# Delta rule and expert layer: first inverse evicted from PSUM by partition quarters, states and scaled values on ScalarE, a new planned order

## The chip, the cores and the metric

The kernel runs on one core of a Trainium2 chip. The metric is device time in microseconds (us) of one execution, as the median of several runs; lower is better. A profiled execution is a separate run in which every instruction's start and end is recorded. It takes a little longer, so its times are compared with its own sum.

The core has a matrix engine (TensorE, PE in the profile; its weight loads are PEld), VectorE (DVE), ScalarE (ACT), GpSimd (POOL) and SyncE (SP). Each engine takes its instructions strictly in the order of its own queue. SP is used here to issue transfers (DMA), as are ScalarE's and GpSimd's queues at places. TensorE's results land in PSUM, 128 partitions with eight banks each, and are copied from there to SBUF by ScalarE or VectorE; such a copy is called an eviction below.

## The reference

Two blocks follow each other, all in float32.

```python
# delta rule: q, k, v are (4, 8, 768, 48), beta is (4, 8, 768)
k_n = k / (norm(k) + 1e-6)
state = zeros((B, H, D, D))
for t in range(S):
    y[:, :, t] = einsum('bhd,bhde->bhe', q[:, :, t], state)
    v_old = einsum('bhde,bhd->bhe', state, k_n[:, :, t])
    state = state + beta[t] * einsum('bhd,bhe->bhde', k_n[:, :, t], v[:, :, t] - v_old)
# experts: x is y with heads joined, (3072, 384); each row goes to the one expert with the largest logit
expert = argmax(x @ w_gate, axis=1); gate = softmax(x @ w_gate)[expert]
out[row] = gate * (relu(x[row] @ w1[expert]) @ w2[expert])   # 8 experts, hidden size 1024
```

## The kernel before

**Tiling.** The 768 steps of a sequence are cut into NT = 12 chunks of C = 64. One *turn* t handles chunk t of all 32 heads at once. Within a chunk the recurrence is a triangular system, so a turn needs the inverse of a unit-like triangular 64 x 64 matrix per head. That inverse is built from two 32 x 32 diagonal blocks (by VectorE) and one block across them (by TensorE).

**Scores.** `scores(t)` multiplies keys with keys and queries with keys. For t >= 2 it does this in two halves of 32 products each (L323, written "half a" and "half b" below), into the PSUM pair BY, which ScalarE evicts into XY (keys with keys, tile blkA) and P (queries with keys, tile pA) before the next half can start. For t < 2 the keys' product comes first, into BY for t = 0 and BZ for t = 1, and is evicted to XY by ScalarE (first bank) and VectorE (second bank); the product with the queries follows later. `dve(1024, ...)` at L355 multiplies P by a mask on VectorE.

**The inverse.** `invert(n)` serves the turns 2n and 2n + 1. Four DMAs copy the diagonal blocks of XY, one 32-partition quarter each, into tile GD (also in blkA); for n = 0 two of them are issued by SP and two by ScalarE. VectorE transposes GD into GL (L378, two instructions), computes norms and factors by Newton steps (L386 to L413; the last writes nt, the inverse norms per token), then does the elimination (L417 to L450, some 95 small instructions) and two transposes into TT (L458). `tmp`, `prod`, `X` and U are its scratch tiles.

**A turn.** `load_kv(t)` loads v and kt and scales v by nt: for t < 2 with 16 ScalarE instructions (L473), else with one VectorE instruction of 768 elements (L476). `turn(t)` puts v into the PSUM pair BR (`values`, L520), adds the state's part (`with_state`, L502), evicts it as R (ScalarE), multiplies with the diagonal blocks (`inverse(0)`, L537), evicts Z (ScalarE), adds the part across (L547), evicts R, multiplies again (`inverse(1)`), evicts Z, and adds keys times Z to the state in PSUM (`kz`, L561). The state is evicted in two halves of 64 partitions each, one by ScalarE and one by VectorE (recorded at L257 and L259, the lines of the helper `copy`), into S, for the next turn. `output(t)` and `logits(t)` compute the chunk's result, store it, and compute the router's logits; `route` computes each row's place in its expert's list, mostly with small VectorE instructions, and scatters the places to HBM.

**Experts.** `early_rows`, `early`, `expert(e)` gather rows by those lists, transpose them (L830), do both layers (L848, L877) and scatter the result. Three weight buffers overlay tiles of the first block (blkA, pA), so the first expert's weights are loaded once the inverses are done.

**The order.** Nothing is ordered by the order of the source. `P.op(engine, cost, fn, r, w, prio, passes)` records a work item with its engine, an assumed cost, what it reads and writes, and a due time (`prio`, in turns). `Plan.order` then replays the items with these costs on a model of the engines: at each step the engine that is free first takes, of what is ready, the item with the lowest due time; items with a due time of at most URGENT (R, Z and S copies) are waited for if they are about to come. LAT is the assumed delay from one engine to another. [...] The instructions are issued in the resulting order, so a changed cost can move any of them on any queue. The Tile layer sets the semaphores from the tiles that the instructions touch.

## Time and profile before

| | us |
|---|---|
| median of 3 runs | 600.73 (600.27 to 600.76) |
| the profiled execution | 616.37 |
| its span, first to last instruction | 614.6 |
| PE busy | 516.0 (84%) |
| DVE busy | 241.7 (39%) |
| ACT busy | 151.2 (25%) |
| mean granted TensorE clock | 0.893 |

How to read it: the span is what the records cover; the profiled execution's own time is 1.8 us longer. Busy time is an average over two quite different parts. Up to about 287 us the turns run, after that the experts. "Idle before" in a timeline line stands in square brackets: how long the engine had done nothing, and which instruction's end let it go on. The list of waits has the columns who waited, for whom, us in total, times, longest. A group line gives line, engine, operation, output and input, shapes, count, busy us and mean ns of one, and idle time before.

### The profile page before, as it was taken

How to read it: one execution, taken by the hardware profiler on the slowest of the kernel's cores; microseconds unless marked ns; L12 is line 12 of the kernel's file. 1: busy time of each engine (PE TensorE's matmuls, PEld its weight loads, DVE VectorE, ACT ScalarE, POOL GpSimd, SP SyncE). 2: the span in 40 equal slices, each digit the busy share in tenths (PEclk: the TensorE clock that was granted, in tenths of full speed). 3: DMA queues.
4: the chain of work that ended last, by engine and by line, in shares of the span. 5: the costliest groups of instructions: out<-in, count | busy, mean ns of one | idle time of the engine just before them, and what ended most of it. 6: DMA issues, size and time to landing. Idle time of an engine off the chain costs nothing. (4 is left out here: it accounts for less than half of the span.)

```text
span 614.6 us, 15547 instructions
## 1 busy us (share of the span) xinstructions
PE 516.0 (84%) x6724; PEld 348.6 (57%) x6725; DVE 241.7 (39%) x957; ACT 151.2 (25%) x297; POOL 111.7 (18%) x118
## 2 busy tenths in 40 slices
PE   3447877889888888868869999999999999999990
PEld 3335665767767777756547455555555555555550
DVE  5795797978979874203101102101021011110100
ACT  2373443544445243321001111101101110101100
POOL 9000000030110301133042302213031130102011
PEclk9975786878969798865988999999999999999996
DMA  7985442434512245011755423314244220000000
GB/s 156 217 200 136 124 121 66 137 97 131 140 34 75 90 149 190 29 28 26 284 192 162 151 103 129 123 57 153 103 152 132 99 77 14 28 1 27 13 22 16
DMA packets 29511, 64.32 MB, mean 105 GB/s; under 512 B 5558, under 2 KB 17766, under 8 KB 29408
## 3 DMA queue, kind: packets, MB, share of 16 engines
q1 hardware_dynamic: 24368, 52.76, 28.7%
q0 software_dynamic: 4416, 9.47, 4.9%
q10 hardware_dynamic: 656, 1.07, 0.8%
q8 instruction: 53, 0.87, 0.6%
q14 instruction: 18, 0.15, 0.1%
HBM read 49.62 MB, written 11.04 MB: 99 GB/s over the span
## 5 line engine op out<-in xcount | busy, mean ns | idle before, releaser
L848 PE MATMUL pair<-kqA,blkA 128*128 128x416 f32 (+2 forms) x288 | 91.6, 477 | 3.2 <-ACT kqA L857 1.6
L877 PE MATMUL pair<-blkA,kqA 128*128 128x384 f32 x240 | 80.0, 491 | 0.0
L848 PEld LDWEIGHTS pair<-kqA,blkA 128*128 128x128 f32 x288 | 55.0, 205 | 37.2 <-issue 28.6
L854 DVE TENSOR_SCALAR kqA<-pair 128x416 f32<-128x416 f32 (+2 forms) x36 | 19.6, 544 | 140.8 <-PE pair L848 85.6
L777 POOL DMA_INDIRECT out<-y,rows_i x30 | 28.9, 962 | 222.0 <-ACT y L868 157.7
L323 PE MATMUL pair<-kqA 48*64 48x128 f32 (+1 forms) x896 | 40.5, 329 | 31.8 <-ACT pA L257 17.2
L877 PEld LDWEIGHTS pair<-blkA,kqA 128*128 128x128 f32 x240 | 45.0, 190 | 34.7 <-issue 5.6
L323 PEld LDWEIGHTS pair<-kqA 48*64 48x64 f32 x896 | 31.9, 181 | 37.8 <-ACT pA L257 17.1
L848 PE MATMUL pair<-kqA,pA 128*128 128x416 f32 x144 | 51.1, 514 | 0.3 <-ACT y L868 0.3
L857 ACT ACTIVATE kqA<-pair 128x416 f32<-128x416 f32 (+2 forms) x36 | 17.2, 478 | 134.0 <-PE pair L848 92.4
L537 PE MATMUL pair<-R,blkA 32*32 32x48 f32 x1536 | 34.4, 241 | 16.8 <-ACT R L257 8.2
L877 PE MATMUL pair<-pA,kqA 128*128 128x384 f32 x144 | 48.1, 491 | 0.0
L865 DVE TENSOR_SCALAR y<-pair,rows 32x384 f32<-32x384 f32 (+1 forms) x15 | 8.5, 607 | 92.8 <-ACT y L868 85.4
L537 PEld LDWEIGHTS pair<-R,blkA 32*32 32x32 f32 x1536 | 29.2, 150 | 22.2 <-ACT R L257 10.1
L848 PEld LDWEIGHTS pair<-kqA,pA 128*128 128x128 f32 x144 | 27.1, 190 | 22.7 <-issue 21.1
L877 PEld LDWEIGHTS pair<-pA,kqA 128*128 128x128 f32 x144 | 26.9, 190 | 21.2 <-issue 3.8
L502 PE MATMUL pair<-S,kqA 112*64 112x96 f32 x704 | 35.3, 259 | 2.8 <-ACT pA L257 1.8
L868 ACT ACTIVATE y<-pair,rows 128x384 f32<-128x384 f32 x15 | 8.7, 580 | 113.9 <-PE pair L877 108.3
L702 POOL DMA_INDIRECT lists<-ent,ri x24 | 24.9, 1038 | 63.2 <-DVE ri L690 27.4
L502 PEld LDWEIGHTS pair<-S,kqA 112*64 112x64 f32 x704 | 32.0, 145 | 4.5 <-ACT pA L257 2.4
L770 POOL DMA_INDIRECT kqA<-xs,rows_i x30 | 29.8, 994 | 24.1 <-DVE rows_i L767 15.3
L257 ACT ACTIVATE blkA<-pair 128x512 f32<-128x512 f32 x22 | 23.3, 1057 | 26.3 <-PE pair L323 24.0
(121 smaller groups left out, 673.6 us busy)
## 6 DMA issues: line engine op xcount, KB each, us to landing
kqA<-in_kq SPq DMA_DIRECT2D x46, 192.0 KB, 4.6
blkA<-in_w SPq DMA_DIRECT2D x15, 512.0 KB, 5.1
blkA<-in_w SPq DMA_DIRECT2D x10, 768.0 KB, 14.4
v<-in_vtok SPq DMA_DIRECT2D x12, 384.0 KB
kt<-in_ktok SPq DMA_DIRECT2D x12, 384.0 KB, 5.5
xs<-x SPq DMA_DIRECT2D x24, 192.0 KB, 2.3
pA<-in_w SPq DMA_DIRECT2D x9, 512.0 KB, 5.4
pA<-in_w SPq DMA_DIRECT2D x6, 768.0 KB, 4.6
```

Source lines behind the costliest of these rows:

```text
L257: return lambda: nc.scalar.activation(out=o, in_=i, func=AF.Copy, scale=scale)
L323: nc.tensor.matmul(bk[bank + e][half(x), i * w : i * w + w].rearrange("p (k c) -> p k c", c=C), lhsT=v[feat(e), 0, x * FQ + f, :], rhs=v[f ...
L502: nc.tensor.matmul(bk[bank + g][half(x ^ g if first else x), 2 * D * i : 2 * D * i + 2 * D], lhsT=KQ(t)[0 : 64 + D, k, x * FQ + f, :], rhs ...
L537: nc.tensor.matmul(at(BZ, f, e)[quad(q)], lhsT=tt[quad(q), :, 16 * u + 8 * e + f], rhs=R[quad(q), f, e, :], start=True, stop=True, skip_gr ...
L702: P.op("POOL", 1.0, lambda i=i: nc.gpsimd.indirect_dma_start(out=lists[i % 2], out_offset=bass.IndirectOffsetOnAxis(ap=ri[:, i : i + 1], a ...
L770: nc.gpsimd.indirect_dma_start(out=dst, out_offset=None, in_=xs, in_offset=bass.IndirectOffsetOnAxis(ap=idx, axis=0), bounds_check=N - 1, ...
L777: nc.gpsimd.indirect_dma_start(out=out, out_offset=bass.IndirectOffsetOnAxis(ap=idx, axis=0), in_=src, in_offset=None, bounds_check=N - 1, ...
L848: nc.tensor.matmul(bk[b][:, 0:n], lhsT=a1[:, s, f * 128 : f * 128 + 128], rhs=xT[:, s, :], start=(s == 0), stop=(s == NK - 1))
L854: (lambda f=f, b=b: nc.vector.tensor_scalar(out=hT[:, f, :], in0=bk[b][:, 0:n], scalar1=0.0, scalar2=None, op0=OP.max))
L857: (lambda f=f, b=b: nc.scalar.activation(out=hT[:, f, :], in_=bk[b][:, 0:n], func=AF.Relu)),
L868: (lambda: nc.scalar.activation(out=y[0:n], in_=bk[b][0:n, 0:DM], func=AF.Copy, scale=gate)),
L877: nc.tensor.matmul(bk[b][:, 0:DM], lhsT=hT[:, f, at : at + 128], rhs=a2[:, f, :], start=(f == 0), stop=(f == NF - 1))
```

## The change

- **First inverse.** For t < 2 the diagonal blocks are evicted straight from PSUM into GD by four instructions of 32 partitions and 512 elements, quarters 0 and 1 by ScalarE, 2 and 3 by VectorE. The four DMAs of `invert(0)` are gone. The evictions into XY for t < 2 remain, all on ScalarE, and are due later (t - 60 instead of t - 94).
- **cnt.** The copy of the constant `first` into cnt moves from VectorE to ScalarE.
- **Scaling of v.** For every turn it is done by 16 ScalarE instructions of 48 elements, each an item of its own, due at t - 1.5 (VP).
- **States.** Both halves of S are evicted by ScalarE.
- **The planner.** It knows a clock: within windows of 3.413 us it adds up how much of TensorE's array is used (`use`), and an item in a window after a slack one costs `cold` times as much. An order dependency (a write after a read) between instructions of one engine has no delay, VectorE's assumed delay is 0.12 instead of 0.16, and several costs differ. So the order changes on all engines.

```diff
+VP = 1.5
+WINDOW, WAKE, STAY = 3.413, 1000, 700
...
-    LAT = {"PE": 0.16, "DVE": 0.16, "ACT": 0.12, "POOL": 0.12, "SP": 2.0}
+    LAT = {"PE": 0.16, "DVE": 0.12, "ACT": 0.12, "POOL": 0.12, "SP": 2.0}
...
+            order.update(self.readers.get(k, ()))
...
+        deps += [(d, 0.0 if self.ops[d][0] == eng and eng != "SP" else
+                  self.LAT[self.ops[d][0]] if self.ops[d][6] is None else self.ops[d][6]) for d in order]
...
+            if passes:
+                while int(t / WINDOW) > window:
+                    fast = used.get(window, 0.0) >= (STAY if fast else WAKE)
+                    window += 1
+                if not fast:
+                    cost *= cold
+                for k in range(8):
+                    w = int((t + cost * k / 8) / WINDOW)
+                    used[w] = used.get(w, 0.0) + use / 8
...
-    P.op("DVE", 0.1, lambda: nc.vector.tensor_copy(out=cnt[:], in_=const("first")), r=["cf"], w=["cnt"], prio=-5)
+    P.op("ACT", 0.2, copy("ACT", cnt[:], const("first")), r=["cf"], w=["cnt"], prio=-5)
...
+            for q in range(4):
+                eng = "DVE" if q > 1 else "ACT"
+                o = GD[quad(q), :, 16 * u : 16 * u + 16]
+                i = pairs[b // 2][quad(q)].rearrange("p e (f c) -> p e f c", c=C)[:, :, :, 32 * (q % 2) : 32 * (q % 2) + 32]
+                if q % 2:
+                    o, i = o.rearrange("p c (e f) -> p c e f", e=2), i.rearrange("p e f c -> p c e f")
+                else:
+                    o = o.rearrange("p c (e f) -> p e f c", e=2)
+                P.op(eng, 1.05, copy(eng, o, i), r=kb(b), w=[("GD", q)], prio=t - 94)
             for e in range(2):
-                P.op("DVE" if e else "ACT", 0.7, copy(
-                    "DVE" if e else "ACT",
+                P.op("ACT", 1.05, copy(
+                    "ACT",
                     xy[:, :, 16 * u + 8 * e : 16 * u + 8 * e + 8].rearrange("p c f -> p f c"),
                     bk[b + e].rearrange("p (f c) -> p f c", c=C)),
-                    r=[("bk", b + e)], w=[("XY", n % 3, u, e)], prio=t - 94)
+                    r=[("bk", b + e)], w=[("XY", n % 3, u, e)], prio=t - 60)
...
         for q in range(4):
             s = q % 2
-            e, k = (nc.scalar, "ACT") if n == 0 and s else (nc.sync, "SP")
-            P.op(k, 0.6, dma(e, flat(GD[quad(q)]), flat(xy[quad(q), 32 * s : 32 * s + 32, :])),
+            if n == 0:
+                continue
+            P.op("SP", 0.6, dma(nc.sync, flat(GD[quad(q)]), flat(xy[quad(q), 32 * s : 32 * s + 32, :])),
...
-        dve(768, lambda: nc.vector.tensor_tensor(
-            out=vs[t % 2][:], in0=vs[t % 2][:],
-            in1=nt[:, u * 16 : u * 16 + 16].rearrange("p (e f) -> p f e", e=2).unsqueeze(3).to_broadcast(
-                [128, FQ, 2, D]), op=OP.mult),
-            [("nt", t // 2 % 3)], [("v", t % 2)], t - 2.5)
+        for i in range(2 * FQ):
+            v = vs[t % 2][:, i % FQ, i // FQ, :]
+            P.op("ACT", 0.225, lambda v=v, i=i: nc.scalar.activation(
+                out=v, in_=v, func=AF.Copy, scale=nt[:, 16 * u + i : 16 * u + i + 1]),
+                r=[("nt", t // 2 % 3), ("v", t % 2)], w=[("vn", t % 2, i)], prio=t - VP)
...
-                q = "DVE" if e else "ACT"
-                P.op(q, 0.83, copy(
+                q = "ACT"
+                P.op(q, 0.78, copy(
```

## The prediction

> **What bounds the kernel now.** I read the stages first. The cuts are the starts of the first inverse product (L537) of turns 0, 2, 4, 6, 8 and 10; the last line is the expert part. Columns: window, length, then busy time (instructions) of PE, PEld, DVE, ACT, POOL, granted clock, DMA share, GB/s.
>
> ```profile
> 47.78:95.09 47.31, 34.17 (x926) 27.49 (x922) 36.05 (x139) 18.65 (x30) 0.31 (x1) 0.72 0.44 121
> 95.09:128.76 33.67, 29.82 (x881) 24.76 (x881) 30.14 (x138) 15.27 (x28) 2.22 (x3) 0.81 0.40 116
> 128.76:166.30 37.54, 32.77 (x917) 26.87 (x913) 31.75 (x140) 18.18 (x33) 5.44 (x6) 0.86 0.41 112
> 166.30:203.14 36.84, 31.55 (x881) 26.42 (x881) 31.79 (x143) 17.20 (x31) 5.72 (x5) 0.86 0.28 82
> 203.14:240.60 37.46, 32.55 (x914) 27.58 (x912) 29.21 (x139) 13.69 (x28) 7.00 (x6) 0.86 0.36 113
> ...
> 287.20:614.60 327.40, 298.92 (x1051) 169.14 (x1051) 38.95 (x83) 34.02 (x68) 62.67 (x64) 0.96 0.29 96
> ```
>
> The last stage is TensorE's own, and the change touches none of it but planner costs. What can move is the recurrence before it: 12 turns, an inverse per two turns. One pair of turns takes 47.3 us, the next four 36.4 on average, the best 33.7. In the long one TensorE is busy for 34.2 of 47.3. The TensorE timeline (start, duration, what, idle before and its releaser) says what it waits for:
>
> ```profile
> 47.78 1.51 PE L537 MATMUL pair<-R,blkA 32*32 32x48 f32 x64
> ...
> 95.09 1.51 PE L537 MATMUL pair<-R,blkA 32*32 32x48 f32 x64 [2.31 <-DVE blkA L458]
> ...
> 128.76 1.45 PE L537 MATMUL pair<-R,blkA 32*32 32x48 f32 x58
> ```
>
> Turn 2 starts when VectorE's last transpose (L458) of the second inverse is done, at 95.0; TensorE had this turn's residual ready on ScalarE at 82.7 and filled part of the 12 us with score products and state products, at a granted clock of about a half. So the question is why VectorE took from 47.4 to 95.0 for an inverse that alone takes 25.75 (first one: transposes at 20.60, last transpose over at 46.35). The list of waits and VectorE's timeline answer:
>
> ```profile
> DVE S L259 <- ACT S L257: 38.8, 7, 14.4
> ```
>
> ```profile
> 8.27 1.04 DVE L259 COPY blkA<-pair 128x512 f32<-128x512 f32 x1 [4.98 <-ACT blkA L257]
> 10.58 4.65 DVE L288 COPY cnt<-cf 128x8 f32<-128x8 f32 x1 [1.27 <-DMA cf<-c_f]
> 10.66 4.57 DVE L259 COPY blkA<-pair 128x512 f32<-128x512 f32 x1
> ...
> 20.60 1.31 DVE L378 STREAM_TRANSPOSE blkA<-blkA 128x512 f32<-128x512 f32 x2 [1.48 <-DMA blkA<-blkA]
> ...
> 60.97 0.96 DVE L259 COPY S<-pair 64x768 f32<-64x768 f32 x1 [6.60 <-ACT S L257]
> ...
> 218.69 0.96 DVE L259 COPY S<-pair 64x768 f32<-64x768 f32 x1 [5.34 <-ACT S L257]
> ```
>
> VectorE stands in its own queue behind its half of the state copy: 6.60 and 2.96 us within the second inverse, 14.9 us in the four pairs after it (3.16, 2.08, 4.28, 5.34), the last 14.4 after all inverses. The state copy waits for TensorE, and TensorE's next even turn waits for the inverse behind the copy.
>
> **The change, part by part.**
>
> *State halves both on ScalarE.* Removes from VectorE per pair 2 x 0.96 (L259 row) and the wait: 3.7 us per pair on average from turn 2 on, 9.6 in the second inverse. Adds to ScalarE one 0.80 copy a turn. On TensorE's path little changes: the two halves already ran one after the other (ScalarE 60.13 to 60.93, VectorE 60.97 to 61.93), so 0.80 + 0.04 + 0.96 becomes 0.80 + about 0.75, a gain of 0.2 a turn, counted as nothing.
>
> *Scaling of v on ScalarE for all turns.* Rows:
>
> ```profile
> L476 DVE TENSOR_TENSOR v<-v,nt 128x768 f32<-128x768 f32 x10 | 9.5, 954 | 0.1
> ...
> L473 ACT ACTIVATE v<-v,nt 128x48 f32<-128x48 f32 x32 | 7.4, 321 | 0.4 <-DVE prod L427 0.4
> ```
>
> VectorE loses 10 x 0.95. ScalarE gains 160 instructions; sixteen in a row took 3.71 (0.232 each), so 3.7 a turn, 7.4 a pair. With the state copies (1.6) ScalarE goes from 17.7 a pair (mean of 18.18 and 17.20 above) to about 26.7 of 34.5. That is cover, not free time: every R and Z copy of the chain is on ScalarE, and one that comes due inside a group of scalings waits up to 0.23. If the planner places them well it costs nothing; if each of the five chain copies of a turn loses a quarter us it costs 1.2 a turn. Queued behind the first scaling of a pair, which waits for nt (4.5 us after the transposes), is the state copy of the even turn.
>
> *VectorE's sum.* Inverse to inverse took (237.4 - 95.04)/4 = 35.6; less 3.7, 1.9 and 1.9 is 28.1. TensorE then sets the pair, at the 33.7 of the pair in which it waited least or somewhat more.
>
> *First inverse.* Removed: four transfers of 128 KB (two on SP's queue, two on ScalarE's) and cnt's copy on VectorE, which held VectorE from 10.58 to 15.23, until GpSimd's memsets ended. Added: eight quarter evictions, four on each engine. The nearest row is the transposing eviction of 512 elements, 1.06 on ScalarE, 1.04 on VectorE; the straight one is 0.62, and I keep 1.06. Two things in the new instruction order matter. cnt's copy now stands on ScalarE ahead of the first quarter, and waits for cf, which lands at 10.58; ScalarE's first eviction was at 7.16. And the quarters wait for each other: ScalarE's second for VectorE's first, VectorE's second for ScalarE's second. The Trainium skill (PSUM — Partial Sum Buffer, "PSUM bank collisions raise a hardware error") lets two engines use different 32-partition quadrants of a bank at once; then four rounds from 10.8 end at 15.0. The row of before speaks otherwise: VectorE's eviction of another bank began at 8.27, 0.04 after ScalarE's ended, and the new order has the same waits. Seven links of 1.08 from 10.8 end at 18.4. I take 18.4 against 20.6; the ends are 15.0 and 18.4 (with 0.62 for half of them about 16.9).
>
> The last transpose of the first inverse comes at 18.4 + 25.75 = 44.2. SP no longer stands behind VectorE from 10.9 to 15.3: the ten issues from there to v took 7.7 us (16.56 to 24.22), so v is issued near 18.6 and lands near 24 (its neighbour took 5.7 from issue to landing; with its old issue time near 30). One rule speaks against: SBUF — State Buffer, "SBUF: two separate sides", says that a VectorE instruction in a two-port mode and a GpSimd one lock each other out. cnt's 4.65 us is that. In the changed kernel the kqA memset (1.81) falls after the first query product, some 21.4, beside the first inverse, so at most 1.8 on it; at 46.5 a memset of 0.95 beside VectorE's mask left that at 1.18, as elsewhere. I take nothing: TensorE isn't at turn 0 before 45 anyhow.
>
> Because: ScalarE makes the four XY copies after the quarters (17.3 to about 21.1), so the query products run at 19.3 and 22.5 (2.0 each, then 1.0 for the copy), the second copy ends at 25.7, and the scores of turn 2 start at 25.9 instead of 21.2. Before, six score halves and the values came ahead of turn 0 (26.6 us); now five, a half costs 3.6, and the 1.6 wait for kq at 21 to 23 falls away: 25.9 + 19 to 21.4, turn 0 at about 45.5 against 47.8. **The edit in the title gains 2.2 us on VectorE and is paid back on ScalarE**; I count 2 us.
>
> *Second inverse.* XY of turn 3 is copied by 42, the four transfers (2.4 to issue, 2.3 to land) by 46.7; VectorE is free at 44.2 and first does four masks of 1.15: transposes at 48.8. Then the order puts turn 4's mask, which waits for a score half that now runs inside turn 0: 45.5 + 1.5 + 1.0 + 1.5 + 2.0 + 1.7 = 53.2, mask over at 54.5. What is left of 25.75 after transposes and four instructions (2.2) is 23.5: **done at 78**. TensorE: from turn 0 to turn 2's residual took 35 us (47.8 to 82.7), plus the score half moved in (2.0), less the stalls around it: ready at about 80. So turn 2 starts at 80 instead of 95.1: 15 us. Ends: 77 (no mask wait) and 86 (v late, opening as slow as before).
>
> *Order with a clock model.* Of itself no instruction more or less; it decides whether TensorE keeps its best pair. Values cost 1.56 in warm windows and 2.9 in half-clock ones. Four pairs of 36.4 become 34.5 (between 33.7 and the 35.6 of VectorE): 4 x 1.9 = 7.6. Ends: 33.7 (10.8) and 38 (loses 6.4), where ScalarE delays a chain copy by 0.25 each time.
>
> *From turn 10 to the end*: 240.6 to 287.2, then the experts. VectorE is nearly idle there, weights 0 load behind the last inverse as before, everything moves with it: nothing gained or lost, give or take 3.
>
> **Sum.** Profiled execution 616.4 (span 614.6): less 15, less 7.6 gives 593.8. The runs' median is 15.6 below the profiled one; the stages that change are the same in both, so 600.7 - 22.6 = 578.
>
> **Rivals.**
> - *ScalarE becomes the bound* (0.12). For: 26.7 of 34.5 us in a queue that runs in order; against: the order puts scalings where ScalarE waited for TensorE. Turn 2's gain stays, pairs take 37.5: 15 - 4.4, time 590.
> - *Slower* (0.06). The state copy of each even turn stands behind the first scaling, which waits for nt. nt comes about 6 us after the inverse is done (mask 1.2, transposes 1.4, 3.4 more), the state is due 10 after: 4 us of slack. If the transfers or a mask make nt later than that by d, all five pairs lose d; past 22.6/5 = 4.5, so nt 14.5 after the inverse, it is a loss. At d = 6: 608. Against: VectorE waited for transfers only at the first inverse (1.48) and one more (0.47).
> - *No change* (0.03): something other than the recurrence, a load of weights, sets 287.2; 600.7. The load of weights 0 ends near 255, so little speaks for it.
> - *More* (0.06): the quarters overlap, v comes early, and the clock stays up, so that values and scores cost 1.5 less a turn: 578 - 3 - 12 = 563.
>
> **How the numbers follow.** The likeliest (0.73) is 578; its own ends are 15 + 10.8 + 3 (572) and 9 + 5 - 3 (590). For 8 in 10 I go from 567, into the case of more, to 591, which holds ScalarE's rival. 0.2% is about what a measurement can tell from no change. Faster 0.73 + 0.06 + 0.11, same 0.03, slower 0.07.
>
> **What would show it.** Turn 2's first inverse product at 80 and no state copy on VectorE; first transposes near 18 and scores of turn 2 near 26, not 21; VectorE idle for masks and transfers instead; ScalarE near 26.7 us a pair; starts of even turns 33.7 to 35.6 apart. Wrong would be: state copies on ScalarE with a wait for scalings ahead of them, VectorE again the last to release L537's successor, or pairs above 37.

## The result: 1.1% faster, a quarter of what was predicted

The kernel before took 600.75 us (median of 4 runs, 600.27 to 601.68), the changed kernel 595.36 us (median of 4, 592.43 to 601.74). The ratio is 0.989, with a 95% interval of 0.985 to 0.993. The prediction was 578 us, with a range of 567 to 591. The sign and the start were right, the size was not: 5.4 us instead of 22.6. With so few runs even the 1.1% is not firm: the kernel before, measured against itself with 4 runs, gave 0.990 (e12 below).

In all that follows a median is over all runs of a kernel, while a ratio leaves out those in the slower of the two states that executions of one kernel fall into, so that the two can differ (in e9 below 607.0 against 598.4 us stands beside a ratio of 1.028).

The runs were made in groups, with the kernel before in each. It took about 600 us here and 598.4 (588 to 603) in one later group, and 615 to 617 us in four other groups, so only runs of one group are compared. The profile from which the prediction was made (616.4 us) is of the second kind. The profile of the changed kernel (596.2 us) is of the first.

The same cut into stages, for the changed kernel: starts of the first inverse product (now L560) of turns 0, 2, 4, 6, 8 and 10, then the experts. Columns as before: window, length, busy time (instructions) of PE, PEld, DVE, ACT, POOL, granted clock, DMA share, GB/s.

```profile
0.00:43.91 43.91, 19.80 (x421) 16.00 (x422) 32.04 (x125) 25.18 (x56) 15.02 (x19) 0.91 0.89 226
43.91:76.58 32.67, 26.82 (x795) 22.34 (x795) 31.08 (x121) 23.27 (x57) 1.34 (x3) 0.76 0.31 90
76.58:119.40 42.82, 37.29 (x946) 32.29 (x945) 33.67 (x154) 26.87 (x67) 3.71 (x5) 0.76 0.40 110
119.40:157.90 38.50, 32.99 (x946) 28.87 (x945) 25.75 (x124) 27.02 (x67) 7.07 (x5) 0.87 0.49 118
157.90:195.96 38.06, 31.87 (x947) 27.75 (x945) 32.91 (x154) 26.65 (x67) 6.83 (x7) 0.91 0.32 91
195.96:229.55 33.59, 30.09 (x914) 25.58 (x913) 24.41 (x126) 21.73 (x62) 4.67 (x5) 0.91 0.46 147
...
273.73:594.40 320.67, 296.33 (x1055) 166.99 (x1054) 39.22 (x84) 34.06 (x68) 62.72 (x64) 0.97 0.29 98
```

Turn 2 starts at 76.6 instead of 95.1: the gap ahead of it is gone. But the four pairs after it take 38.2 us on average (153 in all), where before's profile had 36.4 and 34.5 was predicted. The counts behind PE give one reason, to which the experiments lead: 795 matmuls in the first pair instead of 926, then 946, 946, 947 and 914 instead of 881, 917, 881 and 914. Work moved into the pairs. It is not the only reason, as the last experiments show.

The list of waits says that VectorE no longer stands behind a state copy. It waits instead, with its mask instructions, for ScalarE's evictions of P, and no wait of TensorE for a mask is in the list:

```profile
DVE pA L384 <- ACT pA L276: 18.9, 5, 10.3
```

The opening, on ScalarE, VectorE (start, duration, line, what, idle before and its releaser) and GpSimd:

```profile
10.41 1.02 ACT L276 ACTIVATE blkA<-pair 32x512 f32<-32x512 f32 x1
12.52 1.63 ACT L276 ACTIVATE blkA<-pair 32x512 f32<-32x512 f32 x2 [1.09 <-DVE blkA L278]
```

```profile
11.46 1.02 DVE L278 COPY blkA<-pair 32x512 f32<-32x512 f32 x1 [8.17 <-ACT blkA L276]
13.14 0.70 DVE L278 COPY blkA<-pair 32x512 f32<-32x512 f32 x1 [0.66 <-ACT blkA L276]
...
15.85 0.70 DVE L278 COPY blkA<-pair 32x512 f32<-32x512 f32 x1 [0.66 <-ACT blkA L276]
16.58 1.30 DVE L408 STREAM_TRANSPOSE blkA<-blkA 128x512 f32<-128x512 f32 x2
...
20.48 1.27 DVE L436 TENSOR_SCALAR rt<-rt 128x32 f32<-128x32 f32 x1
```

```profile
19.90 1.81 POOL L1005 MEMSET kqA<- 128x2048 f32 x1 [6.46 <-PE pair L342]
```

The quarters do wait for each other in a chain of seven links, as the row of before had said. The chain starts at 10.41 and ends at 16.55, because half of the quarters take only 0.6 to 0.7 us. The two that overlap (from 13.14 on both engines) belong to different turns, so to different banks. And one instruction that takes 0.18 us elsewhere (L436, at 54.10) took 1.27 us beside GpSimd's memset, and ended with it.

### The profile page after: what moved, and what is told of

It reads as the page before. It is cut to its first block, busy times and chain, and to the rows that moved or that the text cites. A ratio compares the mean times of both kernels' runs of the same rounds, so it can differ in the third digit from the quotient of the medians.

```text
span 594.4 us, 15693 instructions
## 1 busy us (share of the span) xinstructions
PE 509.3 (86%) x6724; PEld 348.2 (59%) x6725; DVE 226.1 (38%) x937; ACT 198.7 (33%) x475; POOL 113.8 (19%) x118
## 5 line engine op out<-in xcount | busy, mean ns | idle before, releaser
L871 PE MATMUL pair<-kqA,blkA 128*128 128x416 f32 (+2 forms) x288 | 89.5, 466 | 2.5 <-DVE kqA L877 1.0
L871 PEld LDWEIGHTS pair<-kqA,blkA 128*128 128x128 f32 x288 | 52.4, 194 | 36.3 <-issue 28.6
L900 PEld LDWEIGHTS pair<-blkA,kqA 128*128 128x128 f32 x240 | 44.9, 190 | 34.8 <-issue 5.6
L342 PE MATMUL pair<-kqA 48*64 48x128 f32 (+1 forms) x896 | 39.9, 340 | 26.3 <-ACT blkA L276 8.7
L342 PEld LDWEIGHTS pair<-kqA 48*64 48x64 f32 x896 | 32.7, 189 | 30.5 <-ACT blkA L276 8.9
L501 ACT ACTIVATE v<-v,nt 128x48 f32<-128x48 f32 x192 | 48.1, 328 | 5.8 <-DMA v<-in_vtok 3.1
L725 POOL DMA_INDIRECT lists<-ent,ri x24 | 26.9, 1120 | 99.2 <-DVE ri L713 42.9
L560 PE MATMUL pair<-R,blkA 32*32 32x48 f32 x1536 | 32.5, 248 | 13.9 <-ACT R L276 7.6
L525 PE MATMUL pair<-S,kqA 112*64 112x96 f32 x704 | 38.0, 270 | 4.4 <-ACT S L276 2.3
L560 PEld LDWEIGHTS pair<-R,blkA 32*32 32x32 f32 x1536 | 28.4, 153 | 18.9 <-ACT R L276 9.2
L900 PEld LDWEIGHTS pair<-pA,kqA 128*128 128x128 f32 x144 | 26.9, 190 | 21.2 <-issue 3.8
L525 PEld LDWEIGHTS pair<-S,kqA 112*64 112x64 f32 x704 | 34.3, 153 | 6.4 <-ACT pA L276 2.2
```

What stands on the lines that cost most here:

```text
L342: nc.tensor.matmul(bk[bank + e][half(x), i * w : i * w + w].rearrange("p (k c) -> p k c", c=C), lhsT=v[feat(e), 0, x * FQ + f, :], rhs=v[f ...
L501: P.op("ACT", 0.225, lambda v=v, i=i: nc.scalar.activation(out=v, in_=v, func=AF.Copy, scale=nt[:, 16 * u + i : 16 * u + i + 1]), r=[("nt" ...
L525: nc.tensor.matmul(bk[bank + g][half(x ^ g if first else x), 2 * D * i : 2 * D * i + 2 * D], lhsT=KQ(t)[0 : 64 + D, k, x * FQ + f, :], rhs ...
L560: nc.tensor.matmul(at(BZ, f, e)[quad(q)], lhsT=tt[quad(q), :, 16 * u + 8 * e + f], rhs=R[quad(q), f, e, :], start=True, stop=True, skip_gr ...
L725: P.op("POOL", 1.0, lambda i=i: nc.gpsimd.indirect_dma_start(out=lists[i % 2], out_offset=bass.IndirectOffsetOnAxis(ap=ri[:, i : i + 1], a ...
L871: nc.tensor.matmul(bk[b][:, 0:n], lhsT=a1[:, s, f * 128 : f * 128 + 128], rhs=xT[:, s, :], start=(s == 0), stop=(s == NK - 1))
```

## The experiments

Theory at the start: VectorE's place behind the state copy caused the gap before turn 2, and without it TensorE sets pairs of about 34 us. Rivals: the execution that was read was not like the timed ones; the new order makes the pairs worse; ScalarE does. Five groups of runs; "before" in each row is the kernel before in that group. With 4 runs a ratio to before resolves no more than about 1%: the kernel before against itself gave 0.990 (0.981 to 0.999) with 4 runs, and 0.999 (0.996 to 1.002) with 20. Each start of a turn below comes from one execution.

| kernel | us (runs) | before | ratio, 95% | turn 0 | turn 2 | turn 10 | experts |
|---|---|---|---|---|---|---|---|
| e1 before | 615.5 (20) | 615.1 | 0.999 (0.996-1.002) | 48.7 | 94.6 | 242.9 | 290.9 |
| e2 state split again | 618.8 (20) | 615.1 | 1.005 (1.002-1.008) | 44.1 | 84.6 | 242.9 | 291.3 |
| e3 v on VectorE | 616.6 (20) | 615.1 | 1.002 (1.000-1.005) | 43.9 | 84.1 | 233.7 | 285.5 |
| e4 clock model off | 606.6 (4) | 615.1 | 0.987 (0.981-0.993) | 44.9 | 79.2 | 233.5 | 280.2 |
| e5 old first inverse | 616.7 (20) | 616.2 | 1.003 (0.999-1.006) | 45.1 | 77.4 | 245.6 | 297.9 |
| e6 order only | 617.1 (20) | 616.2 | 1.003 (1.000-1.006) | 46.3 | 86.0 | 242.2 | 292.4 |
| e7 before, state on ScalarE | 612.2 (12) | 616.2 | 0.996 (0.993-1.000) | 49.3 | 90.9 | 239.2 | 286.9 |
| e8 changed | 617.6 (9) | 616.2 | 1.005 (1.000-1.010) | 45.4 | 78.8 | 238.9 | 290.3 |
| e9 before, scatters held | 607.0 (4) | 598.4 | 1.028 (1.017-1.040) | 47.9 | 93.4 | 227.2 | 267.0 |
| e10 changed, scatters held | 599.1 (4) | 598.4 | 1.015 (1.004-1.027) | 44.1 | 78.6 | 224.2 | 268.9 |
| e11 changed, scatters twice | 609.6 (4) | 598.4 | 1.032 (1.013-1.051) | 44.4 | 77.8 | 233.2 | 281.0 |
| e12 before | 611.5 (4) | 614.7 | 0.990 (0.981-0.999) | 48.6 | 95.2 | 238.1 | 286.0 |
| e13 changed | 618.4 (20) | 614.7 | 1.006 (1.003-1.009) | 44.2 | 78.3 | 242.7 | 294.5 |
| e14 moves, old planner | 611.4 (20) | 614.7 | 0.995 (0.992-0.997) | 43.0 | 81.8 | 230.5 | 278.4 |
| e15 clock model off | 611.4 (4) | 614.7 | 0.989 (0.980-0.999) | 44.8 | 79.9 | 237.0 | 286.7 |
| e16 before, scatters held | 616.5 (20) | 616.7 | 1.000 (0.996-1.003) | 46.5 | 93.0 | 237.6 | 278.0 |
| e17 changed, scatters held | 614.0 (20) | 616.7 | 0.994 (0.990-0.997) | 43.7 | 77.3 | 232.7 | 279.7 |
| e18 old planner, scatters held | 609.7 (14) | 616.7 | 0.989 (0.986-0.993) | 44.1 | 80.3 | 222.7 | 270.6 |

(Start of the turns' first inverse product and of the experts' first product, us, in the profiled execution. "Scatters held": GpSimd's scatters of list entries come later than in the kernel named; there, what lies behind turn 8 carries them.)

**Was the execution that was read an untypical one? (e1)** The kernel before, unchanged.

> The kernel before, unchanged, profiled a second time. The sum of the prediction was made on an execution of 616.4 us, 15.6 us above the median of the runs. Theory A (the read execution was an untypical one): a new profile has a span near 599 us, and one or two stages are shorter than read, so that turn 2 starts 5 us or more before 95.1, or the expert part takes about 320 us instead of 327.4. Theory B (profiling itself costs 15 us, evenly): the span is again near 614, with the same stages. The ratio to the kernel before is 1.000 either way.

The stages came again (45.96, 33.02, 37.37, 40.25, 37.62), and so did the time, 615.5 us. Neither theory of the two holds as put: profiling does not cost 15 us, since the runs around it take 615 us as well (nor does it cost a little always: e3's profiled execution took 613.0 us, its median is 616.6). There are groups of runs in which this kernel takes 615 us, and the prediction mixed the two: stages from one kind, median from the other.

**Which edit closes the gap before turn 2? (e2, e3, e5, e6, e7)** One part undone at a time, or alone.

e2 takes this out of the changed kernel, and e7 puts it alone into the kernel before, the other way round:

```diff
-                q = "ACT"
+                q = "DVE" if e else "ACT"
```

> The changed kernel with the second half of every state copy back on VectorE. If VectorE's place behind the state copy was the cause of the late second inverse: waits of VectorE for ScalarE's half come back (30 us or more in all), turn 2 starts some 8 to 15 us later than 76.6, and the time rises by about 8 to 15 us, to 603 to 610. If the order or the other moves did it: turn 2 stays near 77 and the time within 2 us of 595.

> The kernel before with one edit: both halves of the state copy on ScalarE. By the prediction this alone closes most of the gap: VectorE's 38.8 us of waiting for the state go, the second inverse ends near 80 to 85 and turn 2 starts at 82 to 87 instead of 95, and the time falls by 8 to 15 us. Rival (the gap is given back by TensorE's clock and stalls in later pairs): turn 2 earlier by as much, but the pairs from turn 2 to 10 sum to more than 146, and the time falls by less than 6 us.

e3 has load_kv as in the kernel before:

```diff
-            P.op("ACT", 0.225, lambda v=v, i=i: nc.scalar.activation(
-                out=v, in_=v, func=AF.Copy, scale=nt[:, 16 * u + i : 16 * u + i + 1]),
...
+        dve(768, lambda: nc.vector.tensor_tensor(
+            out=vs[t % 2][:], in0=vs[t % 2][:],
...
```

> The changed kernel with the scaling of v as before (VectorE from turn 2 on, one instruction of 0.95 us; the 3.7 us group on ScalarE for turns 0 and 1). Theory of the prediction (VectorE set the pairs): pairs of turns get about 1.9 us longer, the time rises by about 8 us. Rival (TensorE sets the pairs, and ScalarE's scalings are cover or harm): the time stays within 2 us, or falls by 2 to 5 us, since ScalarE loses about 7 us a pair.

e5 has the first inverse fed as before, two evictions and four transfers, and cnt's copy on VectorE:

```diff
-            if n == 0:
-                continue
+            e, k = (nc.scalar, "ACT") if n == 0 and s else (nc.sync, "SP")
```

> The changed kernel with the first inverse fed as before: two evictions of the query products, four transfers, and the copy of cnt on VectorE. By the prediction the edit gains 2.2 us on VectorE and pays it back on ScalarE: turn 0 starts about 2 us later (46 to 48), turn 2 likewise, and the time rises by about 2 us. Rival (the start is worth more, since all later turns hang on it): first transposes near 20.6, turn 2 4 us or more later, the time 4 us or more above the changed kernel in the same session. Rival (nothing): within 1 us.

e6 keeps of the change only class Plan and the costs:

> The kernel before with only the planner's part of the change: the clock model, the costs and the waits that it reckons with; state halves, scaling of v and first inverse as before. By the prediction this alone shortens the four pairs by part of 7.6 us and leaves the wait before turn 2: turn 2 near 93 to 95, time 3 to 7 us less. Rival (the order harms): pairs after turn 2 longer than in the kernel before (mean above 37.1), time equal or 2 to 6 us more.

In e2 VectorE's wait for the state is back (who waited, for whom, us in total, times, longest):

```profile
DVE S L278 <- ACT S L276: 39.1, 10, 15.3
```

Turn 2 comes 5.8 us later than in e8. The time is 618.8 us beside 617.6 and 618.4 for the changed kernel in the neighbouring groups: a loss of 8 to 15 us is excluded. e3 says the same of the scaling of v: turn 2 comes 5.3 us later, the time is 616.6 us, and the pairs do not get 1.9 us longer each but sum to 149.6 us against 160.1 in e8 (one execution each). So VectorE did not set the pairs. e5 says it of the first inverse: transposes at 18.15 instead of 16.6, turn 2 (77.4) and the time no worse than in e8. Alone, the state copies bring turn 2 only from 95 to 90.9, for a new wait takes the place of the old one. VectorE now stands behind v's transfer (5.61 us of it before turn 2), and the time is 0.4% less, not 8 to 15 us:

```profile
DVE v L476 <- DMA v<-in_vtok: 18.4, 4, 5.8
```

The order alone (e6) brings it to 86.0, which I had not expected, lengthens the pairs to 156.1 us in sum (148.3 in e1), and gains no time. No single part owns the gap. What matters more: turn 2 moved between 77 and 95 us in these kernels and the time moved by 1%, without following it. The expectation that turn 2's gain is kept fell here.

**Is the order from the clock model worth something? (e4, e15, e14)**

```diff
-WINDOW, WAKE, STAY = 3.413, 1000, 700
+WINDOW, WAKE, STAY = 3.413, 0, 0
```

> The changed kernel with the planner's clock model set so that TensorE always counts as fast; the costs and the other moves stay. If the order from the clock model is worth what the prediction gave it (7.6 us over four pairs): the time rises by 5 us or more. If it is worth nothing or harms: within 2 us, or 2 to 5 us less, with the pair from turn 2 to turn 4 shorter than 42.8 us.

> The changed kernel with the clock model off (TensorE always counts as fast), as in the earlier run, now beside the changed kernel itself. There it took 606.6 us where the kernel before took 615.1 and, in another session of the same chip, the changed kernel 617.6. If the clock model's order is the harm: 6 to 11 us below the changed kernel here too, below 590 if the kernel before takes 600. If that gain was a matter of where the scatters fell: within 3 us of the changed kernel.

e14 puts the whole class Plan and the costs of the kernel before under the three moves:

> The moves of the change (quarters, state halves and v scaling on ScalarE) with the planner and the costs of the kernel before. If the order from the clock model makes the pairs long: turn 2 near 76 to 82, pairs sum to 133 to 140, the time 8 us or more below the changed kernel on the same chip. If ScalarE's added work does: pairs as long as in the changed kernel, time within 3 us of it.

With the model off the medians are 8.5 and 3.4 us below the kernel before, and e15's is 7.0 us below the changed kernel of its group (e13), as expected if the clock model's order is the harm. But they come from 4 runs each, which by e12's 0.990 of the kernel before against itself proves little. e14 and e13 have 20 runs each in one group: 611.4 against 618.4 us, ratios 0.995 and 1.006. **The planner's part of the change (clock model, costs and delays together) costs 7.0 us, 1.1%, where the kernel before takes 615 us.** e14 is below both kernels there. Its pairs were not as short as 133 to 140, though (148.7 in sum), and it was not run in a group of the 600 us kind, so whether it beats the changed kernel there is open.

**The changed kernel again (e8, e13) and the kernel before again (e12).**

> The changed kernel once more, beside runs of the kernel before on the same chip. The kernel before ran in 600.7 us in the first session and in 615 us, with the stages of the profile that was read, in the session of the first four experiments. Theory A (the same stages are longer in such a session for both kernels, and the gain read from the trace holds beside it): the changed kernel takes about 592 to 597 us where the kernel before takes 615, a gain of 18 to 23 us. Theory B (the changed kernel has the slower stages too): about 606 to 610 us, the same gain of 1.1%. Theory C (the gap before turn 2 closes, the pairs after it get longer): even turns start near 44, 77 and 119 again, with the pair from turn 2 to turn 4 over 40 us.

> The kernel before, unchanged, profiled a third time. If this falls on a chip where it takes about 600 us: the short stretches of TensorE in turns 4 to 8 are absent, turn 2 still starts at 93 to 96, the four pairs sum to 132 to 138 instead of 145.5, and the expert part with what lies ahead of it takes about 367 us instead of 374. If it takes 615 us again, the stages are those of the first profile.

> The changed kernel, unchanged, beside the run above. Theory (the gap before turn 2 closes and the pairs after it get longer): turn 2 some 15 to 18 us ahead of the kernel before, turn 10 only 3 to 10 us ahead, pairs summing to 145 to 153. The prediction's own step would have needed pairs summing to 138 and a lead of 20 us or more at turn 10.

In both groups the changed kernel is 0.5% slower than the kernel before, and turn 2 still comes 17 us earlier (78.3 against 95.2 in e13 and e12). At turn 10 the lead is gone: 242.7 against 238.1. The pairs sum to 164.4 us against 142.9. Theory C holds; what was a gain in the first group is a small loss here.

**What makes the 615 us? (e9, e10, e11, e16, e17)** In the profile of the kernel before, TensorE in turn 8:

```profile
203.14 1.27 PE L537 MATMUL pair<-R,blkA 32*32 32x48 f32 x48
204.80 0.29 PE L537 MATMUL pair<-R,blkA 32*32 32x48 f32 x3 [0.40 <-issue]
205.54 0.26 PE L537 MATMUL pair<-R,blkA 32*32 32x48 f32 x2 [0.44 <-issue]
206.27 0.33 PE L537 MATMUL pair<-R,blkA 32*32 32x48 f32 x4 [0.47 <-issue]
207.04 0.41 PE L537 MATMUL pair<-R,blkA 32*32 32x48 f32 x7 [0.44 <-issue]
```

and GpSimd at the same time:

```profile
203.51 0.97 POOL L702 DMA_INDIRECT lists<-ent,ri  x1 [15.85 <-DVE rt L396]
204.79 0.97 POOL L702 DMA_INDIRECT lists<-ent,ri  x1 [0.30 <-issue]
206.06 1.74 POOL L702 DMA_INDIRECT lists<-ent,ri  x1 [0.30 <-issue]
208.10 0.97 POOL L702 DMA_INDIRECT lists<-ent,ri  x1 [0.30 <-issue]
```

TensorE runs two to seven matmuls, stops 0.4 us without waiting for anything the profile shows, and so on, while GpSimd issues scatters of list entries. Every profile of the 615 us kind with the scatters in place has this somewhere in turns 4 to 8; the profile of the changed kernel at 596 us has scatters at the same places and none of it. To test it, five groups of scatters are held back, with their entries kept in seven buffers; the aim was to place them behind the last turn's products:

```diff
-                r=[K("ent"), K("ri")], w=[("lists", i % 2)], prio=pr, lat=2.0)
+                r=[K("ent"), K("ri"), ("Z", 1)], w=[("lists", i % 2)], prio=pr, lat=2.0)
+        held.append(place)
+        if m >= CLOSE:
+            while held:
+                held.pop(0)()
```

> The kernel before with the first five groups of list scatters (GpSimd, four at a time, one group every two turns) held back until the last turn's products are done, so that none falls into turns 2 to 10; the result is the same. In the executions with about 615 us TensorE issues two to five matmuls, pauses 0.4 us, and so on, while such a group runs (for instance from 203 to 210 us), and ScalarE and VectorE stand still without a releaser of their own; in the execution of the changed kernel with 596 us this is absent. If the scatters starve the instruction streams: the stretches of two to five matmuls vanish from turns 4 to 8, the pairs from turn 2 to 10 sum to about 138 instead of 145.5, and what is lost comes back after the last turn, since the scatters then stand ahead of the experts. If something else starves them: the stretches stay at the same turns.

> The changed kernel with the same groups of scatters held back. If the scatters hide the change's gain: turn 10 starts near 228 to 230, as in the execution of 596 us, instead of 239, and some 10 us ahead of the kernel before with scatters held back. If the change's order is itself no better in the pairs: turn 10 starts no more than 15 us before that of the kernel before, the lead it had at turn 2, or less.

e11 issues each scatter twice (`for _ in range(2):`):

> The changed kernel with every list scatter issued twice (the second writes the same entries again), so 48 instead of 24; TensorE's order up to the experts is unchanged. If the scatters starve the other engines' instruction streams: each group disturbs about twice as long, turn 10 starts 6 to 10 us later than 238.9 and the time rises by 8 to 20 us. If they don't: turn 10 stays within 3 us and only the last groups, ahead of the experts, add some 3 to 6 us.

These three fell into the one later group in which the kernel before took 598 us. There is no broken stretch in any of them, not even with 48 scatters, so the theory's form of interference is absent there. Whether a milder one remains is not shown. From turn 4 to turn 10 TensorE's stops without a wait sum to 1.1 us in e10, 6.2 in the 596 us execution and 9.7 in e11, single stops of up to 3.5 us, with 8, 11 and 23 scatters begun in that stretch. But all 8 of e10 fall into turns 8 and 9, where neither e10 nor e11 has any such stop, and e17 below has 3.3 us of stops from turn 4 to 8 without a scatter. e11 reaches turn 10 3.7 us later than the 596 us execution (233.2 against 229.6), less than I had expected. What e9 and e10 show is the pairs without broken stretches, from turn 2 to 10: 133.8 us for the kernel before, 145.6 for the changed one. Of the changed kernel's lead of 14.8 us at turn 2, 2.9 us are left at turn 10.

The times of e9 and e10 hold more than the pairs, for the held scatters cost time behind the turns. In e9, as in e16 and e18, TensorE waits 14 us in the experts for the rows that GpSimd gathers; in e10 and e17 it waits 5.6 to 5.7 us there, in the kernel before 2.1. From e16:

```profile
319.59 1.11 PE L837 MATMUL pair<-cf,kqA 128*128 128x128 f32 x4 [14.55 <-DMA kqA<-xs,rows_i]
```

The same two kernels again, with 616.7 us for the kernel before beside them:

> The kernel before with the first five groups of list scatters held back until after the last turn, as in the earlier run where its pairs from turn 2 to 10 summed to 133.8 us. If the kernel before takes about 615 us beside it and the scatters are the cause of that: no stretches of two to five matmuls in turns 4 to 8, the pairs again sum to 133 to 138 instead of 143 to 148, turn 10 starts near 227 to 231; the stretches turn up behind the last turn, beside the scatters. If the scatters are only a coincidence: the stretches stay in turns 4 to 8 and the pairs sum to 143 or more.

> The changed kernel with the scatters held back, where the pairs summed to 145.6 before. If the long pairs belong to the changed kernel's own order and not to chance: 143 to 149 again, also here, and turn 10 within 6 us of the kernel before with scatters held. If they came of that one execution: below 140.

In e16 turns 2 to 7 are clean, and their three pairs take 98.3 us (33.07, 33.52, 31.67), against 110.6 in e1, and the broken stretches now stand from 218 to 227, where the scatters now are:

```profile
216.90 1.27 PE L561 MATMUL pair<-Z,kt 64*48 64x48 f32 x48
218.61 0.32 PE L561 MATMUL pair<-Z,kt 64*48 64x48 f32 x5 [0.43 <-issue]
219.35 0.31 PE L561 MATMUL pair<-Z,kt 64*48 64x48 f32 x5 [0.42 <-issue]
```

```profile
217.38 0.97 POOL L705 DMA_INDIRECT lists<-ent,ri  x1 [0.30 <-DVE blkA L450]
218.76 0.97 POOL L705 DMA_INDIRECT lists<-ent,ri  x1 [0.40 <-issue]
```

They were released earlier than intended (208 us, in turn 8), so the sum to turn 10, 144.6, is not the clean one and the expectation's figure for turn 10 was missed. e17 and e18 show the same: no broken stretch before 209 us, and broken ones beside the scatters after it. That the stretches follow the scatters is shown. Why scatters disturb in some groups of runs and not in others is open: one chip showed both (e9 to e11 and e12 to e15).

That the scatters make the whole of the 15 us is not shown. e16 did not come down to 600 us. At turn 8 it was 14.0 us ahead of e1 (191.3 against 205.3). It lost 8.7 of them in turns 8 and 9, where its scatters now stood, won 7.6 from there to the experts, and lost 10.6 in the experts, where it waited for rows (and where 17 matmuls more of its work fall); 2.3 us were left. And the changed kernel's executions of 617.9 us (e8) and 596.2 us differ by 2.2 us ahead of turn 2, by 7.1 in the pairs, by 7.3 from turn 10 to the experts and by 5.1 in the experts, so only a third of the difference lies in the pairs.

**Where the changed kernel's pairs lose (e16, e17, e18).**

> The moves of the change with the planner and costs of the kernel before, scatters held back. If the order from the clock model makes the pairs long: turn 2 at 77 to 83 and pairs that sum to 132 to 139, so turn 10 at 211 to 220 and some 8 us ahead of the changed kernel with scatters held. If ScalarE's added work does: pairs of 143 or more.

Turns 2 to 7, three pairs without scatters, of the kernel before (e16), the changed one (e17) and the moves with the old planner (e18), columns as in the stage table:

```profile
93.02:191.28 98.26, 86.74 (x2673) 73.31 (x2673) 93.00 (x415) 50.59 (x91) 4.88 (x6) 0.92 0.38 112
```

```profile
77.32:189.71 112.39, 95.58 (x2834) 82.59 (x2832) 90.05 (x422) 80.11 (x201) 3.92 (x5) 0.89 0.40 113
```

```profile
80.28:185.27 104.99, 92.37 (x2772) 78.43 (x2768) 85.81 (x413) 77.24 (x197) 3.92 (x5) 0.91 0.38 109
```

The changed kernel's three pairs take 14.1 us more (11.0 in e10 against e9), which eats all but 1.6 us of the 15.7 us that it leads at turn 2. TensorE's groups in the same window, kernel before, then changed (count, busy and mean, idle before and releasers):

```profile
L502 PE MATMUL pair<-S,kqA 112*64 112x96 f32 x352 | 17.0, 253 | 1.1 <-DVE S L259 0.9 <-ACT pA L257 0.2
L323 PE MATMUL pair<-kqA 48*64 48x128 f32 x320 | 11.9, 281 | 3.9 <-ACT pA L257 2.9 <-issue 0.5 <-ACT x L257 0.5
L561 PE MATMUL pair<-Z,kt 64*48 64x48 f32 x384 | 5.9, 209 | 0.3 <-issue 0.3
L590 PE MATMUL pair<-Z,pA 64*64 64x48 f32 x320 | 5.7, 220 | 0.7 <-ACT between L257 0.7
```

```profile
L525 PE MATMUL pair<-S,kqA 112*64 112x96 f32 x386 | 18.9, 256 | 0.8 <-ACT pA L276 0.8
L342 PE MATMUL pair<-kqA 48*64 48x128 f32 x384 | 15.5, 300 | 3.3 <-ACT R L276 2.0 <-ACT pA L276 1.1 <-issue 0.2
L613 PE MATMUL pair<-Z,pA 64*64 64x48 f32 x384 | 7.9, 234 | 0.0
L570 PE MATMUL pair<-Z,blkA 32*32 32x48 f32 x384 | 7.8, 219 | 5.1 <-issue 5.1
L584 PE MATMUL pair<-Z,kt 64*48 64x48 f32 x384 | 7.4, 243 | 0.0
```

- Scores: 64 matmuls more, 3.6 us; masked products: 64 more, 2.2; state products: 34 more, 1.9; together 7.7. Until turn 2 the kernel before had run 576 score matmuls, 128 masked and 128 state ones, the changed one 512, 64 and 96: the kernel before did them in the wait ahead of turn 2.
- State update (L561, now L584): same count, 1.5 us more.
- These 9.2 us have two parts. At the kernel before's busy time per matmul (11.9/320, 5.7/320 and 17.0/352 us) the added matmuls are worth 5.2 us: **that much work has moved in**. The other **4.0 us** are longer matmuls. At the full granted clock they last as long as before (score 275 ns against 278, update 207 in both), but 192 updates instead of 12, 64 masked products instead of none and 64 scores instead of 8 ran while the granted clock was a half (278, 300 and 424 ns). The mean granted clock is 0.89 against 0.92.
- Stops without a wait: 6.8 us (L570 5.1, L560 1.5, L342 0.2) against 0.8. **6.0 us more.**
- Waits for ScalarE 10.0 against 9.2 us, for VectorE none against 1.4: together 0.6 less.

5.2 + 4.0 + 6.0 - 0.6 = 14.6, against 14.1. Most of the stops fall into the product across the diagonal blocks (L570); e17's TensorE in turn 5:

```profile
132.67 1.13 PE L560 MATMUL pair<-R,blkA 32*32 32x48 f32 x64
133.74 1.15 PE L613 MATMUL pair<-Z,pA 64*64 64x48 f32 x64
134.81 0.43 PE L570 MATMUL pair<-Z,blkA 32*32 32x48 f32 x13
137.17 1.00 PE L570 MATMUL pair<-Z,blkA 32*32 32x48 f32 x51 [1.93 <-issue]
```

Three products of short matmuls now follow on each other, 141 matmuls in 2.6 us, and TensorE then stops. In the kernel before a score product stands between the inverse product and the next (126.09, 127.76, 128.79 in e16), with a wait of half a microsecond. e10 had 2.6 us of such stops in these three pairs, the 596 us execution 8.0, so their size varies. Their cause is open: that TensorE gets its instructions too late is a guess from "issue" and from their place, and no run here tests it.

e18 stands between: pairs of 105.0 us, 324 score but 384 masked and 384 state matmuls, 3.5 us of stops. So of the 14.1 us about half (7.4) belongs to the order that the new planner makes, and half remains with the old one, from one execution each. Turn 2 came as expected for e18 (80.3); turn 10 (222.7) came 10 us ahead of e17 but later than expected, and with scatters in turn 8 the pairs to turn 10 sum to 142.4 us, neither of the two readings. The times go the same way: 0.994 of the kernel before for e17, 0.989 for e18. e17's sum to turn 10 (155.4) missed 143 to 149, also with scatters in turn 8; its lead of 4.9 us over e16 at turn 10 is within the 6 expected.

ScalarE did not become the bound. Its copies do come late at places; ScalarE in e17, and TensorE behind it:

```profile
118.06 1.90 ACT L501 ACTIVATE v<-v,nt 128x48 f32<-128x48 f32 x8
119.87 0.79 ACT L276 ACTIVATE R<-pair 128x768 f32<-128x768 f32 x1
```

```profile
120.71 0.32 PE L560 MATMUL pair<-R,blkA 32*32 32x48 f32 x4 [1.28 <-ACT R L276]
```

R was due behind the second product at 118.3; eight scalings stood ahead of it, 1.5 us, not the 0.23 that I had taken. TensorE had a score product to run in between, up to 119.4, and then stood 1.28 us for R.

## Why the prediction was wrong, point by point

- *First inverse.* Predicted: transposes at 18.4, or 16.9 with the short evictions; measured 16.6. The end that I named was right, the value taken was not. The Trainium skill (PSUM — Partial Sum Buffer, "PSUM bank collisions raise a hardware error") lets two engines use different quadrants of one bank at once, but that did not decide: the quarters of one bank waited for each other, so no run here shows it. Turn 0 came at 43.9 against 45.5 predicted, and e5 (1.003 beside 1.005 for e8) shows no gain in time from the edit, so "paid back" held in the time.
- *GpSimd's lock on VectorE* (the Trainium skill, SBUF — State Buffer, "SBUF: two separate sides"). I took nothing, bounded by 1.8. The instruction at 20.48 lost 1.1 us (1.27 instead of 0.18), as the rule would have it. The row that I set against the rule, a mask, was another kind of instruction (TENSOR_TENSOR, not TENSOR_SCALAR). The loss is inside the range that I had left for it.
- *Second inverse and turn 2.* Predicted 80, measured 76.6. Right in so far as VectorE was late and turn 2 came earlier. But the wait at the state copy alone was not the cause: undoing any one part left turn 2 at 77 to 85, and that part alone brought it to 90.9.
- *"Order with a clock model ... Four pairs of 36.4 become 34.5"*: **this is the step that failed, twice.** Its start, 36.4, had the broken stretches beside the scatters in it; without them the pairs of the kernel before take 33.4 (e9, 133.8/4), less than I predicted for the changed kernel. Its end took the work of a pair as given ("of itself no instruction more or less"). But I had written of the gap before turn 2 that TensorE "filled part of the 12 us with score products and state products", and then counted the 15 us of the gap as won. The filling has to run somewhere: 5.2 us of it in three pairs. The other 10 us, longer matmuls at half the granted clock and stops without a wait, had no term in the sum at all. The term of -7.6 us measured +11.8 (145.6 - 133.8, e10 and e9), while the term of -15 us measured -14.8 in the same two.
- *"The stages that change are the same in both"*: not so as far as the runs tell, and the same error seen from the sum. Of the 15.6 us between the profiled execution and the median, the pairs without broken stretches would explain 11.7 (145.5 - 133.8). That is argued from e9: the kernel before itself was not profiled in a group of the 600 us kind.
- *The sum by what was measured:* 600.75, less 14.8 at turn 2 (e9 and e10), plus 11.8 in the pairs, gives 597.8; the runs say 595.4. The rest, 2.4 us, is not settled. It is smaller than what the experts' part varied by between profiles without held scatters, 321 to 328 us. That part was longer where more of it ran at half the granted clock: 4.3 us of 320.7 in the changed kernel's profile, 8.1 of 325.8 in e8, 11.6 of 327.4 in the profile of before (all up to 570 us).
- *ScalarE.* 26.7 us a pair predicted, 26.9, 27.0, 26.7 and 21.7 measured. The rival "ScalarE becomes the bound" had the pairs nearly right (37.5 against 38.2) and the reason wrong, so that was luck. VectorE stopped being waited for, as predicted; that gained 1.4 us in three pairs, since TensorE had hardly waited for it there.
- *"pairs above 37"* was named as a sign of being wrong, and it is the one that came.

## What to carry to other kernels

A gap of the bounding engine is worth its length less the work that was run in it: count the instructions per stage on both sides before calling the gap a gain, and see at which granted clock they will run. When a profiled execution is longer than the timed runs, find where, before a stage table is made from it; here stops of two to five matmuls with no releaser gave it away. And an edit that leaves the count of instructions alone may still order short ones so densely that the engine stops for no wait that the profile shows (6.8 us in three pairs against 0.8).

## What the runs showed of the hardware

- Beside GpSimd's indirect scatters, some 1 us each, TensorE's instruction stream can break up into two to seven matmuls per 0.73 us, and the stretches move when the scatters are moved (e16 to e18). ScalarE can stand still with them: 5.5 us in turn 11 of e8 with no releaser on this core, 3.0 of it after the product that it was to copy had ended. The four profiles without broken stretches (the 596 us one, e9, e10, e11) have no such wait of ScalarE ahead of the experts; of those with broken stretches, e7 has none either. In the groups of runs that show it, the kernel before takes 615 us, in the others 600; one chip showed both.
- TensorE stopped up to 3.5 us inside a product, with no wait in the profile. The sum of such stops in turns 2 to 7 differed between executions of one order of products (2.6 us in e10, 6.8 in e17, both without scatters there).
- The granted clock was at its full value or at a half for stretches of 3.4 us and multiples of it. At a half the same matmul took 1.3 to 1.7 times as long (update 278 ns against 207, values 867 against 500).
- Holding the scatters back made the kernel before 2.8% slower (1.7 to 4.0) in the group in which they do not disturb, and left it unchanged (1.000) in one in which they do. In both, TensorE then waited over 14 us for gathered rows in the experts.
